# Expert 0's first part cut at 256 columns and five slices in place of 192 columns and six

## The chip, the cores and the metric

The kernel runs on one core of a Trainium2 chip. The metric is device time in microseconds (us), the median of several executions. One further execution was profiled; its trace gives a start and an end for every instruction of every engine. TensorE is PE in the rows (PEld is its weight load), VectorE is DVE, ScalarE is ACT, GpSimd is POOL, and SyncE, which issues plain DMAs, is SP.

## The reference

Three stages follow one another, on 4 batches of 768 tokens.

```python
for t in range(S):                       # gated linear attention, 8 heads of 48
    state = alpha[:, :, t, :, None] * state + einsum('bhd,bhe->bhde', k[:, :, t], v[:, :, t])
    y[:, :, t] = einsum('bhd,bhde->bhe', q[:, :, t], state)
...
expert_idx = argmax(x @ w_gate, axis=1)  # 8 experts, one per token, x is (3072, 384)
for e in range(E):
    h = maximum(x[mask] @ w1[e], 0.0)    # 384 -> 1024
    out[mask] = gate_w[mask, None] * (h @ w2[e])   # 1024 -> 384
...
h = x @ w_in                             # 384 -> 2048
g = h * (1.0 / (1.0 + exp(-h)))
return g @ w_out                         # 2048 -> 384
```

## The kernel before

**Stages.** The attention runs first, batch by batch. While the last batch is in work, the routing of the first three is known; the kernel uses that to start expert 0 early. Then come experts 0 to 7, the other seven in an order by their token counts, and then the dense layer.

**One slice of an expert.** The hidden 1024 columns are cut into 8 slices of 128 (`NF`). For a slice `t`, `F1(t, c0, c1)` makes the first products: nine matmuls (three 128-row pieces of the input, three terms each, because every operand is kept as a high part and a low part), each over the token columns `c0` to `c1`. ScalarE then writes the high part of the result, `hh` (L1276), and VectorE the low part, `hl` (L1278). `S1(t, c0, c1, between)` makes the second products: three output blocks `dc` of three matmuls. `between` holds steps that are put into PE's order behind the blocks `dc` 0, 1 and so on.

**Expert 0 in two parts.** A first part covers the first `CA` token columns, which can be gathered from the rows of the first three batches (`gather_a`, two indirect DMAs of POOL, `xg<-x_d,gidx_a`). It runs for the first `part` slices while the last batch is still being routed: its logits are turned, chosen, ranked, and turned into a list of tokens (`pt`, L884, on PE; `tab` and `gidx`, L894 and L895, on VectorE). Then the rest of expert 0's tokens is gathered (`gather(0, ...)`, `xg<-x_d,gidx`). The second part covers the columns from `CA` on for the same slices, and all columns for the slices that are left. With `part = NF - 2` and `CA = 192` that is six slices of 192 columns, the same six again on the rest, and two slices on all. The width of the rest follows the token count: `sized` branches to the smallest of the widths in `ARMS[0] = [424, 448]` that holds it.

**Tiles of tokens.** The gathered rows are turned by PE 128 at a time (`x_tile`, `x_rows`: three transposes `xt` or `both` at L373, the high part `xh` by ScalarE at L377, the low part `xl` by VectorE at L378). Tile 0 and the first 64 rows of tile 1 are turned in the last attention step; the other rows of tile 1 (its first 64 columns are skipped), tile 2 and tile 3 in the first part's last slices. VectorE also turns the counts into an order of the experts (`turns`, L902 to L919) and the lists into that order (`in_turn`, L925 to L932).

**Order.** Each engine runs its instructions in the order in which the program writes them; waits between engines are by semaphores. Before the second part, `hold()` has VectorE clear the ends of three PSUM banks (`hp`, L1263); the second part's first product writes the first of them.

Of the kernel before, what the change touches and what calls it, by code (L numbers as in the profile page):

```python
# [33 lines left out]
NF = DFF // 128  # L34
# [11 lines left out]
    [344, 356, 368, 384],  # L46
    [326, 342, 354, 370],
]
CA = 192
NTILE = NT // 128  # L50
RING = 5
TB = NTILE // B
# [187 lines left out]
def gla_moe_kernel(  # L240
# [32 lines left out]
    def bank(i, shape, name):  # L273
        if i > 1:
            return ps.tile(shape, F32, tag=f"B{i}", name=name)
        if "t" not in both:
            both["t"] = two_banks("both")
        n = 1
        for x in shape[1:]:
            n *= x  # L280
        t = both["t"][: shape[0], i, 0:n]
        return t.rearrange("p (a b) -> p a b", a=shape[1]) if len(shape) == 3 else t
# [60 lines left out]
    def w_rest(t, eng=nc.vector):  # L343
        hi, lo = wslot[slot1(t)]
        eng.tensor_tensor(lo, raw.pop(t), hi.bitcast(F32), op=ALU.subtract)  # L345

    def w_split(t, eng=nc.vector):
        w_cast(t)
        w_rest(t, eng)
# [12 lines left out]
    def gather_rows(x, src, idx, i, n):  # L362
        nc.gpsimd.indirect_dma_start(  # L363
            out=x[:n],
            out_offset=None,
            in_=src,
            in_offset=bass.IndirectOffsetOnAxis(ap=idx[:n, i : i + 1], axis=0),
        )

    def x_rows(g, xs, kt, r0, n, t):  # L370

        for kc in range(KD):
            nc.tensor.transpose(  # L373
                t[:, kc, :n].bitcast(F32R), g[:n, kc * 128 : (kc + 1) * 128].bitcast(F32R), identr[:n, :n]
            )
        xh, xl = (x[:, :, 128 * kt + r0 : 128 * kt + n] for x in xs)
        nc.scalar.copy(xh, t[:, :, r0:n])  # L377
        nc.vector.tensor_tensor(xl, t[:, :, r0:n], xh.bitcast(F32), op=ALU.subtract)  # L378
# [26 lines left out]
    with actx:  # L405
# [528 lines left out]
        def rows(b, c):  # L934
            t = bank(xbank(), [128, 4, PA], "Xt")
            for i in range(4):
                nc.tensor.transpose(t[:, i, :], xb[b][:, i, c * CH : (c + 1) * CH], ident[:PA, :PA])  # L937
            xr = xp.tile([128, 4, 2, D], F32, tag="xr", name="xr", bufs=4)
            src = bass.AP(tensor=t.tensor, offset=t.offset, ap=[t.ap[0], [PA, 4], [64, 2], [1, D]])
            nc.scalar.activation(xr, src, AF.Copy, scale=gate[b][:, c : c + 1])  # L940
            r0 = b * S + c * CH
            nc.sync.dma_start(x_d[r0 : r0 + CH, :], xr.rearrange("p i h e -> p (i h e)"))

        def gather_a():
            nc.vector.tensor_scalar(gidx_a, tab[:, 0:2], float(NT - S - 1), None, op0=ALU.min)
            nc.vector.tensor_scalar(fl[:, 3:4], carry[0:1, 0:1], float(CA), None, op0=ALU.is_lt)
            for kt in range(2):
                gather_rows(XG[kt], x_d[: NT - S], gidx_a, kt, min(128, CA - 128 * kt))

# [86 lines left out]
        for p in range(NP + 1):  # L1036
# [49 lines left out]
            if not on:  # L1086
                x_rows(XG[0], XS[0], 0, 0, 128, bank(2, [128, KD, 128], "xt"))
                x_rows(XG[1], XS[0], 1, 0, CA - 128, bank(0, [128, KD, 128], "xt"))
                w_rest(1)
# [40 lines left out]
    with mctx:  # L1130
# [5 lines left out]
        def gather(e, kts=range(4)):  # L1136
            if e < E:
                for kt in kts:
                    if 128 * kt < CAPS[e]:
                        gather_rows(XG[kt], x_d, gidx, 4 * e + kt, min(128, CAPS[e] - 128 * kt))  # L1140

        def x_tile(e, kt, r0=0, bk=7):
            if e < E and 128 * kt < CAPS[e]:
                n = min(128, CAPS[e] - 128 * kt)
                x_rows(XG[kt], XS[e % 2], kt, r0, n, bank(bk, [128, KD, 128], "xt"))
# [99 lines left out]
        def F1(t, c0, c1, mid=()):  # L1245
            F1_bank(t, c0)
            F1_products(t, c0, c1, mid)
            F1_inner(t, c0, c1)
# [8 lines left out]
        def hold():  # L1257

            HB[0] = -1
            for i in HBS:  # L1260
                held.append(bank(i, [128, CAP], "hp"))
            for t in held:
                nc.vector.memset(t[:, min(ARMS[0]) - CA :], 0.0)  # L1263

# [46 lines left out]
        def S1(t, c0, c1, between=()):  # L1311
            S1_products(t, c0, c1, S1_begin(t, c0), between)

        def S1_begin(t, c0):
            if t == 0 and c0 == 0:
                for dc in range(KD):
                    yb[dc] = bank(dc, [128, CAP], "yb")
            return hq.pop((t, c0))

        def S1_products(t, c0, c1, inner, between=()):  # L1320
            f = t % NF
            wh, wl = wslot[slot1(t)]
            hh, hl = inner
            for dc in range(KD):
                c = 384 + dc * 128
                i = 0
                for a, b_ in ((wh, hh), (wl, hh), (wh, hl)):
                    nc.tensor.matmul(  # L1328
                        yb[dc][:, c0:c1],
                        lhsT=a[:, c : c + 128],  # L1330
                        rhs=b_[:, : c1 - c0],
                        start=(f == 0 and c0 == 0 and i == 0),
                        stop=(f == NF - 1 and i == 2),
                    )
                    i += 1
                if dc < len(between):
                    between[dc]()
# [4 lines left out]
        digits, hots, invert, add = last_tb  # L1342
        row = [lambda c=c: rows(b, c) for c in range(NC)]
# [5 lines left out]

        F1(0, 0, CA, [last["l_turn"], last["l_rows"], l_max, w_diff, *last["weigh"]])  # L1350
        for step in choose:
# [4 lines left out]
            3: [last["turns"]],  # L1356
            4: [last["in_turn"]],
        }
        part = NF - 2
        seq = [(t, CA, CAPS[0]) for t in range(part)] + [(t, 0, CAPS[t // NF]) for t in range(part, E * NF)]  # L1360
        for t in range(part):
            if t == 2:
                add()
                nc.vector.tensor_copy(regs[:, 8:9], carry[:, 0:1])
                w_split(4)
                gather(0, (1, 2, 3))
            if t == 3:
                w_split(5)
            if t + 1 < part:
                F1(t + 1, 0, CA)  # L1370
            for step in beside.get(t, []):
                step()
            if t == part - 2:
                x_tile(0, 1, CA - 128)
            if t == part - 1:
                x_tile(0, 2, bk=4)
            S1(t, 0, CA, ([row[2], ranks_and, row[4]], [lambda: None, invert])[t] if t < 2 else [])
            if t == 0:
                row[5]()
                for step in placed:  # L1380
                    step()
        HBS.append(3)
        hold()
        x_tile(0, 3)
        for t in range(4, 6):
            next_load()
        soon = [6, 7]
# [329 lines left out]
```

## Time and profile before

| | |
|---|---|
| median of 3 runs | 756.24 us (756.05 to 758.76) |
| the profiled execution | 755.89 us, of which its span is 753.9 us |
| PE busy | 741.4 us, 98% of the span |
| granted TensorE clock | 0.999 of full speed over the span |
| first part of expert 0 | from about 126.8 to 146.1 us of the span |

Times in rows are counted from the start of the span. PE is busy nearly all the time, so a stretch of PE that grows or shrinks shows in the total; where PE stands idle in this part of the program, the row after the gap says in brackets how long and for whom.

### The profile page before, as it was taken

To read this page: it belongs to the slowest core of one execution; us is meant where nothing else is said; L and a number is where in the kernel's file an instruction comes from. 1 tells how busy PE (TensorE), PEld (TensorE's weight loads), DVE (VectorE), ACT (ScalarE), POOL (GpSimd) and SP (SyncE) were. 2 spreads that over 40 slices of the span, in tenths; PEclk is the share of its full clock that TensorE was granted. 3 is DMA by queue.
4 is the path that set the end of the run, shared out by engine and by line. 5 is a ranking of instruction groups with operands and counts; after the bars stand their busy time and mean duration, and the time that the engine had idled before them with its cause. 6 is when DMAs were issued, how large, how long until landed. Compare 5 with 4: busy or idle time off the path is not lost.

```text
span 753.9 us, 13462 instructions
## 1 busy us (share of the span) xinstructions
PE 741.4 (98%) x5018; PEld 681.7 (90%) x5018; DVE 464.8 (62%) x779; ACT 366.5 (49%) x685; POOL 163.9 (22%) x206
## 2 busy tenths in 40 slices
PE   8999999999999999999999999999999999999996
PEld 6888888999999999998999999999999999899996
DVE  8999986758778788988786424433342433334222
ACT  2656566445556555656444334544554545324222
POOL 6774321422224223112121200200020020002002
PEclk9999999999999999999999999999999999999999
DMA  9798994544665566563201200030030000001001
GB/s 239 196 225 220 228 275 152 168 143 154 190 198 180 178 191 209 183 188 111 83 24 38 78 19 1 33 83 19 1 110 25 20 30 13 1 1 43 1 0 47
DMA packets 41803, 81.00 MB, mean 107 GB/s; under 512 B 5696, under 2 KB 19999, under 8 KB 41704
## 3 DMA queue, kind: packets, MB, share of 16 engines
q1 hardware_dynamic: 37704, 67.60, 31.1%
q0 software_dynamic: 4000, 12.03, 5.2%
q8 instruction: 68, 1.11, 0.6%
q14 instruction: 31, 0.25, 0.1%
HBM read 68.04 MB, written 9.47 MB: 103 GB/s over the span
## 4 chain that ended last, share of the span: by engine, by line
PE 87%; issue 4%; DVE 3%; ACT 2%; DMA 2%; POOL 1%; POOLq 0%; SPq 0%; DVEq 0%; ACTq 0%
PE hp L1238 37%; PE both L1535 12%; PE ob L1535 12%; PE both L1328 9%; PE yb L1328 4%; PE Ap L607 2%; PE Yp L690 2%; PE Yp L705 2%; PE Lw L535 1%; DMA x_d<-xr 1%; PE xt L373 1%; PE Tp L595 1%; ACT Sb L679 1%; PE Xt L937 1%; PE U L643 1%
## 5 line engine op out<-in xcount | busy, mean ns | idle before, releaser
L1238 PE MATMUL hp<-xh,wh 128*128 128x512 f32 (+10 forms) x498 | 179.9, 364 | 0.4 <-ACT xh L377 0.4
L1238 PE MATMUL hp<-xh,wl 128*128 128x512 f32 (+10 forms) x498 | 179.7, 363 | 0.0
L1512 DVE TENSOR_TENSOR sg<-hp,sg 128x512 f32<-128x512 f32 (+1 forms) x97 | 66.5, 686 | 128.4 <-ACT sg L1511 127.9
L1238 PE MATMUL hp<-xl,wh 128*128 128x512 f32 (+10 forms) x498 | 127.1, 363 | 0.0
L1511 ACT ACTIVATE sg<-hp 128x512 f32<-128x512 f32 (+1 forms) x97 | 57.6, 594 | 118.3 <-PE hp L1238 113.4
L1238 PEld LDWEIGHTS hp<-xh,wh 128*128 128x128 f32 x498 | 93.6, 188 | 11.7 <-issue 0.6
L1238 PEld LDWEIGHTS hp<-xh,wl 128*128 128x128 f32 x498 | 93.7, 188 | 10.5
L1238 PEld LDWEIGHTS hp<-xl,wh 128*128 128x128 f32 x498 | 90.1, 188 | 11.8
L1557 POOL DMA_INDIRECT out_dram<-o,sidx x24 | 23.3, 972 | 275.4 <-ACT o L1555 270.9
L1165 POOL TENSOR_TENSOR wl<-dx,wh 128x384 fp32r<-128x384 f32 x32 | 39.4, 1232 | 166.4 <-ACT wh L1162 166.4
L345 DVE TENSOR_TENSOR wl<-raw,wh 128x768 fp32r<-128x768 f32 x64 | 65.1, 1019 | 8.6 <-ACT wh L341 8.2
L1276 ACT ACTIVATE hh<-hp 128x464 fp32r<-128x464 f32 (+9 forms) x70 | 34.0, 487 | 72.3 <-PE hp L1238 64.9
L341 ACT CAST wh<-raw 128x768 fp32r<-128x768 f32 x64 | 52.0, 831 | 8.6 <-DMA raw<-in_wt_dram 8.5
L1523 DVE TENSOR_TENSOR hl<-sg,hh 128x512 fp32r<-128x512 f32 x49 | 33.9, 693 | 35.6 <-ACT hh L1522 34.2
L1278 DVE SCALAR_TENSOR_TENSOR hl<-hp,hh 128x464 fp32r<-128x464 f32 (+9 forms) x70 | 38.0, 549 | 28.7 <-ACT hh L1276 28.6
L1522 ACT CAST hh<-sg 128x512 fp32r<-128x512 f32 x49 | 30.4, 621 | 49.9 <-DVE sg L1512 38.3
L1523 DVE TENSOR_TENSOR xl<-sg,xh 128x512 fp32r<-128x512 f32 (+1 forms) x48 | 32.7, 681 | 31.7 <-ACT xh L1522 23.3
L1328 PE MATMUL both<-hh,wh 128*128 128x396 f32 (+9 forms) x140 | 47.5, 339 | 0.0
L1522 ACT CAST xh<-sg 128x512 fp32r<-128x512 f32 (+1 forms) x48 | 29.3, 611 | 35.1 <-DVE sg L1512 35.1
L1328 PE MATMUL both<-hl,wh 128*128 128x396 f32 (+9 forms) x140 | 45.8, 327 | 0.5 <-DVE hl L1278 0.5
L1328 PE MATMUL both<-hh,wl 128*128 128x396 f32 (+9 forms) x140 | 45.7, 326 | 0.0
L363 POOL DMA_INDIRECT xg<-x_d,gidx x29 | 33.5, 1155 | 42.6 <-PE xt L373 18.2
(366 smaller groups left out, 1640.8 us busy)
## 6 DMA issues: line engine op xcount, KB each, us to landing
raw<-in_wt_dram SPq DMA_DIRECT2D x64, 384.0 KB, 3.8
raw<-in_w_dram SPq DMA_DIRECT2D x32, 384.0 KB, 3.8
raw<-in_alpha_dram SPq DMA_DIRECT2D x16, 336.0 KB, 3.2
x_d<-xr SPq DMA_DIRECT2D x24, 192.0 KB, 2.8
E<-in_q_dram SPq DMA_DIRECT2D x18, 144.0 KB, 5.0
E<-in_k_dram SPq DMA_DIRECT2D x18, 144.0 KB, 3.5
E<-E POOLq DMA_DIRECT2D x18, 114.0 KB, 6.4
E<-in_q_dram SPq DMA_DIRECT2D x4, 336.0 KB, 8.7
```

Source lines behind the costliest of these rows:

```text
L341: nc.scalar.copy(wslot[slot1(t)][0], raw[t])
L345: eng.tensor_tensor(lo, raw.pop(t), hi.bitcast(F32), op=ALU.subtract)
L1165: nc.gpsimd.tensor_tensor(r["lo"], r["x"], r["hi"].bitcast(F32), op=ALU.subtract)
L1238: nc.tensor.matmul(hp, lhsT=a[:, kc * 128 : (kc + 1) * 128], rhs=x[:, kc, c0:c1], start=(i == 0), stop=(i == 8))
L1276: nc.scalar.activation(hh[:, :n], hp, AF.Relu)
L1278: nc.vector.scalar_tensor_tensor(hl[:, :n], in0=hp, scalar=0.0, in1=hh[:, :n].bitcast(F32), op0=ALU.max, op1=ALU.subtract)
L1328: nc.tensor.matmul(yb[dc][:, c0:c1], lhsT=a[:, c : c + 128], rhs=b_[:, : c1 - c0], start=(f == 0 and c0 == 0 and i == 0), stop=(f == NF - ...
L1511: nc.scalar.activation(sg[:, z], hp[:, z], AF.Sigmoid)
L1512: nc.vector.tensor_tensor(sg[:, z], hp[:, z], sg[:, z], op=ALU.mult)
L1522: nc.scalar.copy(hh[:, z], sg[:, z])
L1523: nc.vector.tensor_tensor(hl[:, z], sg[:, z], hh[:, z].bitcast(F32), op=ALU.subtract)
L1535: nc.tensor.matmul(yb[tt], lhsT=a[:, tt * 128 : (tt + 1) * 128], rhs=b_[:, 384:768], start=(f == 0 and i == 0), stop=(f == NF2 - 1 and i = ...
```

## The change

`CA` goes from 192 to 256, and the first part from six slices to five (`part = NF - 3`). Tile 1 is now gathered as 128 rows by `gather_a` and turned once, in the attention's last step (`min(128, CA - 128)`, `x_rows(XG[1], ..., 0, CA - 128, ...)`, both unchanged in the text). `gather(0, ...)` fetches two tiles in place of three. Tile 3 is turned behind the first block of the last second products, and so before `hold()`. The list of pairs of slices that follows has 64 entries as before, five of them narrow in place of six.

```diff
-CA = 192
+CA = 256
...
-        part = NF - 2
+        part = NF - 3
         seq = [(t, CA, CAPS[0]) for t in range(part)] + [(t, 0, CAPS[t // NF]) for t in range(part, E * NF)]
         for t in range(part):
             if t == 2:
                 add()
                 nc.vector.tensor_copy(regs[:, 8:9], carry[:, 0:1])
                 w_split(4)
-                gather(0, (1, 2, 3))
+                gather(0, (2, 3))
...
-            if t == part - 2:
-                x_tile(0, 1, CA - 128)
+            among = [row[2], ranks_and, row[4]] if t == 0 else [lambda: None, invert] if t == 1 else []
             if t == part - 1:
                 x_tile(0, 2, bk=4)
-            S1(t, 0, CA, ([row[2], ranks_and, row[4]], [lambda: None, invert])[t] if t < 2 else [])
+                among = [lambda: x_tile(0, 3)]
+            S1(t, 0, CA, among)
             if t == 0:
                 row[5]()
                 for step in placed:
                     step()
         HBS.append(3)
         hold()
-        x_tile(0, 3)
```

VectorE, before, from the `hl` of slice 4's first products to the clearing of the banks (`xl_108` is expert 0's low part, `128x3x64` a tile of 64 rows):

```order
L1278 SCALAR_TENSOR_TENSOR hl<-hp,hh 128x192
L902 SCALAR_TENSOR_TENSOR key<-carry,keys 128x8
...
L919 CAST regs<-rk 128x8
L1278 SCALAR_TENSOR_TENSOR hl<-hp,hh 128x192
L925 TENSOR_TENSOR mt<-tab,turn 128x256
L931 TENSOR_REDUCE ttab<-mt 128x32
L932 TENSOR_SCALAR gidx<-ttab 128x28
L378 TENSOR_TENSOR xl_108<-xt,xh_107 128x3x64
L378 TENSOR_TENSOR xl_108<-xt,xh_107 128x3x128
L1263 MEMSET hp 128x232 x3
L378 TENSOR_TENSOR xl_108<-xt,xh_107 128x3x64
```

VectorE at the same place in the change:

```order
L1278 SCALAR_TENSOR_TENSOR hl<-hp,hh 128x256
L902 SCALAR_TENSOR_TENSOR key<-carry,keys 128x8
...
L919 CAST regs<-rk 128x8
L925 TENSOR_TENSOR mt<-tab,turn 128x256
L931 TENSOR_REDUCE ttab<-mt 128x32
L932 TENSOR_SCALAR gidx<-ttab 128x28
L378 TENSOR_TENSOR xl_108<-xt,xh_107 128x3x128
L378 TENSOR_TENSOR xl_108<-xt,xh_107 128x3x64
L1263 MEMSET hp 128x296 x2
```

The `hl` of slice 5 and the turn of tile 1's second half are gone; the low part of tile 3 now stands ahead of the clearing, and all of it still behind `turns` and `in_turn`.

PE, before, at the end of the first part (in brackets what an instruction waits for; `both` and `yb` are the banks of the second products):

```order
L1328 MATMUL yb<-hl,wh_2027 128x192
L373 MATMUL xt<-identr,xg_2042 128x64 [waits DMASW6_49,DVE_49]
L373 MATMUL xt<-identr,xg_2042 128x64 x2
L1289 TENSOR_LOAD regs [waits DVE_49]
L1289 ISA x2
L1295 COMPARE_AND_BRANCH
L1238 MATMUL hp<-xh_107,wh_98 128x232 [waits DVE_49,Activation_49]
...
L1238 MATMUL hp<-xl_108,wh_98 128x232 [waits DVE_49]
```

PE at the same place in the change:

```order
L373 MATMUL xt<-identr,xg_2041 128x128 [waits DMASW4_49,PE_49]
...
L373 MATMUL xt<-identr,xg_2042 128x64 [waits DMASW5_49,PE_49]
L373 MATMUL xt<-identr,xg_2042 128x64 x2
L1328 MATMUL both<-hh,wh_2025 128x256
...
L1328 MATMUL yb<-hl,wh_2025 128x256
L1289 TENSOR_LOAD regs [waits DVE_49]
L1289 ISA x2
L1295 COMPARE_AND_BRANCH
L1238 MATMUL hp<-xh_107,wh_98 128x168 [waits DVE_49,Activation_49]
```

Tile 3's transposes moved up by six matmuls; the second part's first product, 168 columns wide, has one wait for VectorE at its head, and the later wait for the low part, at the `xl` products, is gone.

## Rows read from the trace of the kernel before

**Rows 1.** The page, busy time by engine (us, share of the span, instructions)

```profile
PE 741.4 (98%) x5018; PEld 681.7 (90%) x5018; DVE 464.8 (62%) x779; ACT 366.5 (49%) x685; POOL 163.9 (22%) x206
```

**Rows 2.** Busy time in stretches of the span, granted clock as PEclk

```profile
core 0: us, PE busy (x) PEld busy (x) DVE busy (x) ACT busy (x) POOL busy (x), PEclk, DMA share, GB/s
126.80:146.10 19.30, 18.70 (x170) 16.91 (x169) 13.84 (x49) 9.13 (x21) 4.55 (x5) 1.00 0.44 143
146.10:165.00 18.90, 18.88 (x151) 18.78 (x152) 10.93 (x29) 8.70 (x17) 7.85 (x8) 1.00 0.52 164
165.00:333.00 168.00, 168.00 (x982) 165.46 (x981) 137.00 (x233) 95.51 (x179) 45.39 (x38) 1.00 0.59 185
```

**Rows 3.** The chain in order of time: start, length, what

```profile
125.00 0.35 PE both L373 x3
...
136.55 0.60 PE pt L884 x6
...
137.55 1.00 PE hp L1238 x9
...
145.75 0.33 ACT xh L377
...
146.12 3.28 PE hp L1238 x27
...
151.69 2.01 PE hp L1238 x18
...
156.25 2.72 PE hp L1238 x18
...
360.58 4.12 PE hp L1238 x18
```

**Rows 4.** POOL's timeline, the gathers (start, length)

```profile
122.14 0.94 POOL L363 DMA_INDIRECT xg<-x_d,gidx_a  x1 [0.30 <-issue]
138.51 0.96 POOL L363 DMA_INDIRECT xg<-x_d,gidx  x1 [15.44 <-DVE wl L345]
139.78 1.68 POOL L363 DMA_INDIRECT xg<-x_d,gidx  x1 [0.30 <-issue]
```

**Rows 5.** DMA issues, windows at 122, at 138.5 and at 142 us

```profile
xg<-x_d,gidx_a POOLq DMA_INDIRECT x1, 2.7
...
xg<-x_d,gidx POOLq DMA_INDIRECT x1, 4.0
...
xg<-x_d,gidx POOLq DMA_INDIRECT x1, 2.7
```

**Rows 6.** Busy tenths of the DMA engines, 122 to 126 us, 0.1 us each

```profile
DMA  0000099952395210046844100000003399679799
```

**Rows 7.** VectorE's timeline, 137 to 147 us

```profile
137.41 0.17 DVE L895 TENSOR_SCALAR gidx<-tab 128x4 uint32<-128x4 f32 x1
...
140.97 0.36 DVE L1278 SCALAR_TENSOR_TENSOR hl<-hp,hh 128x192 fp32r<-128x192 f32 x1 [0.33 <-ACT hh L1276]
141.25 0.16 DVE L902 SCALAR_TENSOR_TENSOR key<-carry,keys 128x8 f32<-128x8 f32 x1
...
142.72 0.17 DVE L919 CAST regs<-rk 128x8 int32<-128x8 f32 x1
142.98 0.36 DVE L1278 SCALAR_TENSOR_TENSOR hl<-hp,hh 128x192 fp32r<-128x192 f32 x1
...
144.35 0.18 DVE L932 TENSOR_SCALAR gidx<-ttab 128x28 uint32<-128x28 f32 x1
144.44 0.99 DVE L378 TENSOR_TENSOR xl<-xt,xh 128x192 fp32r<-128x192 f32 x2
145.47 0.75 DVE L1263 MEMSET hp<- 128x232 f32 x3
```

**Rows 8.** ScalarE's timeline, 142 to 147 us

```profile
143.08 0.32 ACT L377 CAST xh<-xt 128x192 fp32r<-128x192 f32 x1
```

**Rows 9.** PEld's loads of the first products, one line, 127 to 146 us (ns min/median/max)

```profile
L1238 PEld LDWEIGHTS hp<-xh,wh x18: 186/192/192, 128.2 to 141.8; 128*128 128x128 f32 x18
```

## The prediction

> **What bounds the kernel now.** I read the page first, then the stretches of the span, then the chain in order of time around expert 0's first part, and last the timelines of the engines that PE waits for there. The page says PE: it is busy 98% of the span [rows 1]. The stretches say where it isn't. From 165 us on, and already from 146.1 to 165, PE is busy in all but 0.02 us of its time; in the first part of expert 0, from 126.8 to 146.1, it lacks 0.6 us of 19.3 [rows 2]. So this is a kernel in which a microsecond more of PE work behind 146 us shows as a microsecond of time, and in which the first part can be shortened only as far as PE isn't made to wait there for somebody else. The clock is granted in full in all these stretches (1.00, the 2.4 GHz level) and plays no part.
>
> The chain shows what PE's time is made of. Nine first products of 192 columns take 1.00 us, 111 ns each; eighteen of 232 columns take 2.01 us, 112 ns each [rows 3]. Forty columns more cost nothing: both widths stand on a floor. The eighteen at 156.25 are nine of 232 and nine of 424 columns and take 2.72 us, so a 424-wide one is (2.72 - 9 x 0.112) / 9 = 0.190 us; one of 512 columns is 4.12 / 18 = 0.229 us [rows 3]. Above the floor a column costs (229 - 190) / 88 = 0.44 ns.
>
> At the end of the first part PE waits until 146.12: the chain goes through ScalarE's `xh` of tile 3 at 145.75 [rows 3]. VectorE is hardly less late there. ScalarE has the high part of tile 1 ready at 143.08 + 0.32 = 143.40 [rows 8], but VectorE comes to its low part only at 144.44, because `turns` (141.25 to 142.89) and the steps of `in_turn` (up to 144.53) stand ahead of it in its order; the clearing of the banks then runs from 145.47 [rows 7].
>
> **The change, part by part.** The sum goes along the time at which the second part's first product can start: 146.12 before [rows 3]. All of PE's work behind it is then compared.
>
> *Tile 1 gathered whole.* The second gather of `gather_a` starts at 122.14 and lands 2.7 us later, at 124.84 [rows 4, 5]; PE's transposes of it are in the chain at 125.00 [rows 3], so there is next to no slack. It now moves 128 rows. POOL's own time is the same (0.94 us for 64 rows, 0.96 for 128 [rows 4]). Bounds for the landing: nothing, and the 4.0 us that the 128-row gather at 138.51 took, that is +1.3 us [rows 4, 5]. In between, the busy tenths show the first gather's 128 rows as a burst of ten slices and the second's 64 rows as one of six, of 0.1 us each [rows 6], so 64 rows more are 0.4 us. I take **+0.4 us**, being the row of this very place. All of the last attention step, the logits and the routing stand behind it.
> By the Trainium skill ("DMA: Bandwidth & Descriptors", section on the anatomy of one SWDGE DMA) a DMA takes about 2.0 us plus its bytes over 436 GB/s; by an estimate from that page 98 KB more cost 0.23 us, and the total would be 0.2 us lower. Its 2.2 us for 64 rows is under the 2.7 us measured here, so the trace decides.
>
> *256 columns in place of 192.* No row has this width. Bounds: the floor of 112 ns, and the 190 ns of 424 columns. The line through 424 and 512 gives 190 - 168 x 0.44 = 116 ns, which I take: **+4 ns** a matmul. Ahead of the list of tokens (`pt`), 27 are on the path (six ahead of the turned logits, 21 between the routing's last transposes and `pt`; while the routing runs on VectorE and ScalarE the others only fill PE): +0.11 us. Behind `pt` come 30 up to the end of slice 4's first products: +0.12 us.
> The Trainium skill ("TensorE: Matmul & The Clock Gate", section on the back-to-back issue gap) gives an isolated matmul N/2.4 + 2.5 ns; by an estimate from that page 256 columns are 109 ns, under this trace's floor, and the total would be 0.2 us lower. For 512 columns it gives 216 ns where the row has 229, so I stay with the line.
>
> *VectorE's queue at the end of the first part.* This is where the gain should come, and where I think it goes. Before, `hl` of slice 4 ends at 140.97 + 0.36 = 141.33 [rows 7]. Now it ends later by 0.4 + 0.11 + 0.12, and by about 0.06 each for `hh` and `hl` that are a third wider (an estimate from the 0.36 us of this `hl`): 142.08. Behind it, in VectorE's order: `turns`, 1.56 us (141.33 to 142.89); `in_turn`, 1.19 us (from 143.34, the end of slice 5's `hl`, which is now gone, to 144.53); the low parts of tiles 2 and 3, a pair of the same sizes as the pair at 144.44, 0.90 us (144.53 to 145.43); the first clearing, 0.04 + 0.25 us, with 296 columns for 232 some 0.07 more [rows 7]. That makes 142.08 + 1.56 + 1.19 + 0.90 + 0.36 = 146.09, and with 0.04 us to start, **146.13**. The second part's first product waits for the clearing at its head. So the start stays where it was.
>
> *What PE does meanwhile.* It loses a slice: 18 matmuls of 111 ns, 2.0 us, and one turn of a half tile. `pt` ends at 137.15 + 0.51 = 137.66 [rows 3]. With 39 matmuls of 116 ns it is at tile 2's transposes at 142.2. Tile 2's gather starts 0.93 us behind `gidx` as before (137.58 to 138.51), at 139.02, and lands 2.7 to 4.0 us later, 141.7 to 143.0; tile 3's starts 1.27 us behind it and lands from 143.0 on [rows 4, 5, 7]. PE is through by about 144.6 and then stands for 1.5 us, where it stood for 0.4 before. Any wait for tiles 2 and 3 up to that size is hidden under VectorE's queue.
>
> *Slice 5 goes whole to the second part.* Its 18 matmuls there have 424 columns in place of 232: 18 x (190 - 112) = **+1.40 us**. The other five narrow slices have 168 columns for 232, both on the floor (192 and 232 are [rows 3]): nothing. PE is full there [rows 2], so all of this shows.
>
> *Steps at nothing.* The 128-row transposes, `xh` and `xl` of tile 1 in the attention's last step lengthen ScalarE and VectorE by 0.1 to 0.2 us where both wait for PE; one gather less on POOL brings tiles 2 and 3 up to 1.27 us sooner, which counts for nothing as long as VectorE's queue is the later one.
>
> Sum: 755.89 (the profiled execution) + 0.01 + 1.40 = 757.3. The median of the runs is 0.35 above the profiled one, so **757.5 us**, 0.2% up. What a measurement of this kernel can tell from no change is about 0.5%, 3.8 us: no change.
>
> **The rivals.** *Early start.* The clearing doesn't hold the product's head (it writes columns from 168 on, the product those below): then only the seventh matmul waits, for the low part at 145.73, the first six take 0.67 us, and the start comes at 145.1: 1.0 us less, 756.5. For it: the columns don't overlap in the narrower arm. Against it: in the order of the change the one wait for VectorE stands at the head. With a gather that lands no later it would be 756.1.
>
> *Late gather.* The whole tile 1 lands 1.0 to 1.3 us later rather than 0.4, as the 4.0 us row has it [rows 5]; this moves everything: 0.6 to 0.9 more, 758.3. For it: two of the three landings shown are 2.7 and both are of 64 rows. Against: the burst in [rows 6].
>
> *Wide matmul off the floor*, the slower side. A load of weights takes 192 ns [rows 9] and is hidden only because the next one begins under the matmul. If 256 columns broke this overlap, a narrow matmul would cost the 190 ns of the nearest row. Ahead of slice 4's `hl` stand 45 first and 27 second products, 72 x 74 ns = 5.3 us: about 762.8, 0.9% slower. It decides from (3.8 - 1.3) / 72 = 35 ns on, a pace of about 150 ns. Against it: 192 and 232 columns share one pace under the same loads, and 424 lies on a line with 512.
>
> *The change doesn't do what it says*, in that the shorter first part starts nothing earlier, is my forecast itself.
>
> **How the numbers follow.** Forecast 0.62 (757.0 to 758.0); early start 0.18; late gather 0.14; wide matmul 0.04; 0.02 for what I don't see. The range that leaves out no more than 2 in 10 goes from the early start with its lower bound to the late gather with a run's spread: 755.6 to 759.2. Faster by over 0.5% would need 752.4, where none of these ends: 0.01. Slower by over 0.5% is the wide matmul and a part of the unseen: 0.05. Same: 0.94.
>
> **What would show it.** Right: VectorE without a gap from slice 4's `hl` to the first clearing, the second part's first product within 0.3 us behind that clearing, near 146.1, and PE idle for 1 to 2 us ahead of it; 256-wide nines of about 1.04 us; tile 1's transposes about 0.4 us later; one more nine of 424 columns. Wrong: a first product that starts ahead of the clearing (early start); nines of 1.3 us or more (wide matmul); a gap of PE ahead of tile 1's transposes of a microsecond (late gather); or PE waiting for tiles 2 and 3 beyond VectorE's queue.

## The result, and the profile after

| | before | changed |
|---|---|---|
| median | 757.26 us (22 runs, 755.0 to 761.4) | 766.71 us (22 runs, 757.1 to 771.4) |
| ratio | | 1.0089, 95% interval 1.007 to 1.0108 |
| granted TensorE clock, mean over a run | 0.997 to 1.0 (its runs beside the experiments) | 0.999 to 1.0 in 4 runs, 0.984 to 0.988 in 18 |
| the profiled execution | 755.89 us | 768.97 us, span 767.3 us, clock 0.986 |

The change makes the kernel 0.9% slower (9.4 us by the medians), where no change was forecast. The 22 runs fall in two groups with nothing between: four at 757.1, 757.8, 758.7 and 759.3 us, near the forecast of 757.5, and eighteen from 763.5 us on, with a median of 767.2. The mean clock parts them without exception. (Four of the eighteen, from 769.0 us on, are left out of the ratio as disturbed; their clock is that of the other fourteen.)

First the page of the changed kernel: PE's busy time as in [rows 1], and the granted clock in 40 slices of the span, 19 us each.

```profile
PE 749.3 (98%) x4997; PEld 690.1 (90%) x4997; DVE 464.5 (61%) x777; ACT 366.3 (48%) x683; POOL 160.4 (21%) x205
...
PEclk9999999869999999999999999999999999999999
```

PE is busy 7.9 us longer with 21 instructions fewer. The clock line says where to look: one slice of 8 and one of 6, between 134 and 173 us, and nothing else. The stretches of that place, as in [rows 2]:

```profile
core 0: us, PE busy (x) PEld busy (x) DVE busy (x) ACT busy (x) POOL busy (x), PEclk, DMA share, GB/s
126.80:144.00 17.20, 17.13 (x165) 15.46 (x164) 12.02 (x37) 10.18 (x22) 1.91 (x2) 1.00 0.48 152
144.00:148.20 4.20, 2.67 (x20) 2.11 (x19) 3.87 (x14) 0.80 (x2) 0.81 (x1) 1.00 0.12 28
148.30:168.70 20.40, 20.34 (x95) 20.28 (x96) 7.05 (x22) 4.43 (x10) 5.93 (x8) 0.50 0.43 140
168.80:200.00 31.20, 31.20 (x175) 29.97 (x174) 20.43 (x35) 15.84 (x29) 4.82 (x5) 1.00 0.42 131
```

In the 4.2 us at the end of the first part PE works 2.67 us. Then the granted clock is 0.50, the lower of the two levels (1.2 GHz), for 20.4 us, although PE is busy in 20.34 of them. PE's timeline at both ends of this stretch (start, length, line, shape, and in brackets the idle time ahead of a row and who ended it):

```profile
130.61 0.38 PE L1238 MATMUL hp<-xh,wh 128*128 128x256 f32 x1
...
145.55 0.42 PE L373 MATMUL xt<-identr,xg 128*128 128x128 f32 x3 [0.98 <-DMA xg<-x_d,gidx]
...
147.37 0.28 PE L1328 MATMUL yb<-hl,wh 128*128 128x256 f32 x1
148.36 0.48 PE L1238 MATMUL hp<-xh,wh 128*128 128x168 f32 x1 [0.71 <-DVE hp L1263]
148.64 0.41 PE L1238 MATMUL hp<-xh,wl 128*128 128x168 f32 x1
148.85 0.41 PE L1238 MATMUL hp<-xh,wh 128*128 128x168 f32 x1
...
166.88 0.63 PE L1238 MATMUL hp<-xh,wh 128*128 128x424 f32 x1
...
168.37 0.53 PE L1238 MATMUL hp<-xh,wh 128*128 128x424 f32 x1
168.72 0.37 PE L1238 MATMUL hp<-xh,wl 128*128 128x424 f32 x1
...
175.96 0.35 PE L1238 MATMUL hp<-xh,wh 128*128 128x420 f32 x1
```

PE stands 0.98 us for the gathered rows of tile 2, works 2.1 us, stands 0.71 us for VectorE's clearing, and its next product already runs at the lower level. From there a product of 168 columns starts every 0.21 us (148.64 to 148.85), nearly twice the 111 ns of [rows 3]. This goes on through all the narrow slices. Only with the first products of 424 columns, from 166.88 on, does the clock come back, at 168.7.

What it costs is read between two points that both kernels have: the second part's first product and the first product of the next expert, 420 columns wide. In the changed kernel that is 175.96 - 148.36 = 27.60 us. The timeline of before has

```profile
128.16 0.36 PE L1238 MATMUL hp<-xh,wh 128*128 128x192 f32 x1
...
162.83 0.35 PE L1238 MATMUL hp<-xh,wh 128*128 128x420 f32 x1
```

and so 162.83 - 146.12 = 16.71 us [rows 3]. Of the 10.9 us more, 1.4 were forecast for slice 5; some 9.4 are the clock. The two groups of runs differ by nearly as much: their medians, 758.3 and 767.2 us, are 9 us apart.

VectorE's timeline of the changed kernel at the same place, as in [rows 7]:

```profile
143.95 0.42 DVE L1278 SCALAR_TENSOR_TENSOR hl<-hp,hh 128x256 fp32r<-128x256 f32 x1 [0.48 <-ACT hh L1276]
144.29 0.16 DVE L902 SCALAR_TENSOR_TENSOR key<-carry,keys 128x8 f32<-128x8 f32 x1
...
147.03 0.81 DVE L378 TENSOR_TENSOR xl<-xt,xh 128x384 fp32r<-128x384 f32 x2
147.91 0.94 DVE L1263 MEMSET hp<- 128x296 f32 x3
```

No row after the first has a wait: the queue runs through from slice 4's `hl` to the clearing, as the prediction described it. From the first product of expert 0 to the second part's first product the changed kernel takes 148.36 - 130.61 = 17.75 us, the kernel before 146.12 - 128.16 = 17.96 us.

### The profile page after: what moved, and what is told of

Its sections match the earlier page's. It is cut to its first block, busy times and chain, and to the rows that moved or that the text cites. A ratio compares the mean times of both kernels' runs of the same rounds, so it can differ in the third digit from the quotient of the medians.

```text
span 767.3 us, 13412 instructions
## 1 busy us (share of the span) xinstructions
PE 749.3 (98%) x4997; PEld 690.1 (90%) x4997; DVE 464.5 (61%) x777; ACT 366.3 (48%) x683; POOL 160.4 (21%) x205
## 4 chain that ended last, share of the span: by engine, by line
PE 81%; DMA 6%; DVE 5%; issue 4%; ACT 2%; SPq 1%; POOL 1%; POOLq 0%; DVEq 0%; ACTq 0%
PE hp L1238 37%; PE both L1534 12%; PE ob L1534 12%; PE both L1328 9%; PE yb L1328 4%; DMA E<-E 2%; PE Ap L607 1%; DVE Pf L562 1%; DMA E<-in_q_dram 1%; PE Yp L690 1%; DMA a__148<-in_alpha_dram 1%; PE xt L373 1%; PE Yp L705 1%; DMA x_d<-xr 1%; DVE Rv L580 1%
## 5 line engine op out<-in xcount | busy, mean ns | idle before, releaser
L1238 PE MATMUL hp<-xh,wh 128*128 128x512 f32 (+10 forms) x495 | 183.0, 371 | 0.7 <-DVE hp L1263 0.7
L1238 PE MATMUL hp<-xh,wl 128*128 128x512 f32 (+10 forms) x495 | 182.6, 370 | 0.0
L1238 PE MATMUL hp<-xl,wh 128*128 128x512 f32 (+10 forms) x495 | 128.7, 369 | 0.0
L1238 PEld LDWEIGHTS hp<-xh,wh 128*128 128x128 f32 x495 | 95.5, 193 | 12.2 <-issue 1.5
L1238 PEld LDWEIGHTS hp<-xh,wl 128*128 128x128 f32 x495 | 95.6, 193 | 10.6
L1238 PEld LDWEIGHTS hp<-xl,wh 128*128 128x128 f32 x495 | 91.7, 192 | 11.9
L1328 PE MATMUL both<-hh,wh 128*128 128x404 f32 (+9 forms) x138 | 48.4, 351 | 0.0
L1328 PE MATMUL both<-hl,wh 128*128 128x404 f32 (+9 forms) x138 | 46.6, 338 | 0.4 <-DVE hl L1278 0.4
L1328 PE MATMUL both<-hh,wl 128*128 128x404 f32 (+9 forms) x138 | 46.5, 337 | 0.0
L363 POOL DMA_INDIRECT xg<-x_d,gidx x28 | 30.8, 1098 | 55.9 <-PE xt L373 25.2
```

Source lines behind the costliest of these rows:

```text
L1238: nc.tensor.matmul(hp, lhsT=a[:, kc * 128 : (kc + 1) * 128], rhs=x[:, kc, c0:c1], start=(i == 0), stop=(i == 8))
L1328: nc.tensor.matmul(yb[dc][:, c0:c1], lhsT=a[:, c : c + 128], rhs=b_[:, : c1 - c0], start=(f == 0 and c0 == 0 and i == 0), stop=(f == NF - ...
```

## The experiments

Two things meet at the place where the clock falls: PE has stood longer than before, and what follows is 168 columns wide where it was 232. The first theory was the first alone: the stands let the clock fall. The rivals were the narrow products alone, and the five slices with their tight gathers. Times in the text are medians; "before" is the kernel before in runs beside them on the same chip.

**Both stands filled** (`filled`). The changed kernel with matmuls of ones that nothing reads, on 128 columns, put into the two stands.

```diff
+        def fill(n):
+            t = bank(3, [128, 128], "fill")
+            for _ in range(n):
+                nc.tensor.matmul(t, lhsT=ones, rhs=ones, start=True, stop=True)
...
+                fill(20)
                 x_tile(0, 2, bk=4)
...
+        fill(18)
         HBS.append(3)
         hold()
```

> The change, with 20 and 18 matmuls of ones by ones (128 columns, result unused) put into PE's order where it waits at the end of the first part: ahead of tile 2's transposes, and behind the last second products. Theory (PE's standing at the end of the first part is what brings TensorE's clock down to its lower level for 20 us): PE has work there, the granted clock stays at full speed, and the time is that of the sum in the prediction, 757 to 758.5 us. Rival (the clock falls because the second part's products have only 168 columns, so the array has less to do between loads of weights): those products are the same here, the clock falls as in the change, about 766 us.

766.68 us (9 runs, before 757.27; ratio 1.0095, 1.0058 to 1.0131): four runs of 759.7 to 761.4 us at a clock of 0.996 to 1.0, five of 766.7 to 768.6 us at 0.988 to 0.991. Five of nine against eighteen of 22 doesn't show that the filling made the fall rarer. What the fallen runs say of the stands can be read only from a profile of one of them (below).

**256 columns, but six slices** (`six256`). All of the change except the number of slices; its second part is 168 columns wide six times.

```diff
-        part = NF - 3
+        part = NF - 2
```

> The change with six slices in the first part in place of five, all else as in the change: 18 matmuls of 256 columns more (2.1 us) ahead of the tiles of the last batch. Theory (standing): the gathers and VectorE are done when PE comes, PE stands for less than 0.5 us, the clock stays at full speed, 756 to 758 us. Rival (168 columns): six narrow slices of 168 columns in the second part, more than in the change; the clock falls, 766 us or more.

757.22 us (10 runs, before 757.27; ratio 0.9994, 0.9974 to 1.0013), clock 0.996 to 1.0 in all of them. The stretch of the second part in its profile:

```profile
145.20:164.00 18.80, 18.64 (x149) 18.49 (x150) 10.64 (x30) 8.02 (x17) 7.38 (x9) 1.00 0.53 170
```

PE stood only once, 0.34 us, ahead of that stretch. Narrow products alone don't bring the clock down here. The wider columns, tile 1 gathered whole and tile 3 turned early together cost nothing that shows.

**192 columns, but five slices** (`five192`). The kernel before with `part = NF - 3`, and nothing else of the change.

> The kernel before with five slices in the first part in place of six, 192 columns kept. Theory (standing): PE comes 2 us earlier to tile 1's transposes, whose gather lands at 142.5 us, and stands some 1.9 us there and some 0.8 us ahead of the second part; the clock falls for about 20 us and the time is 766 to 769 us. Rival (168 columns): the second part has 232 columns as before, the clock stays, about 757.5 us.

760.19 us (10 runs, before 757.27; ratio 1.0031, 1.0012 to 1.0049), clock 0.993 to 1.0. The stretches of its profile:

```profile
142.00:149.00 7.00, 4.42 (x37) 3.88 (x36) 5.69 (x18) 1.45 (x4) 4.37 (x4) 1.00 0.50 146
149.00:165.00 16.00, 16.00 (x128) 15.66 (x128) 9.36 (x25) 6.68 (x14) 6.50 (x8) 1.00 0.52 160
```

PE stood for 2.6 of the 7.0 us at the end of the first part, more than in the changed kernel (1.12, 0.45, 0.21 and 0.81 us), and the clock stayed at 1.00. The time expected of the stands (766 to 769 us) did not come: stands alone don't cost 9 us here, and neither do five slices. Shorter falls are likely in other runs of it, since in six of the ten the mean clock was 0.993 to 0.995. Its second part is 232 columns wide.

**A longer stand in the kernel before** (`idle4`). Four clearings of a 128x512 tile by VectorE ahead of the clearing of the banks.

```diff
+        late_clear = mp.tile([128, TM], F32, tag="sg", name="late_clear", bufs=2)
+        for _ in range(4):
+            nc.vector.memset(late_clear, 0.0)
         HBS.append(3)
         hold()
```

> The kernel before with four clearings of an unused tile of 512 columns on VectorE ahead of the clearing of the PSUM banks; PE's own work is unchanged. VectorE is 1.2 to 2.1 us later there and PE stands for 1.3 to 2.2 us in place of 0.4. Theory (standing): the clock falls, 765 to 769 us, some 10 us more than the 0.9 to 1.8 us that the delay itself costs. Rival (168 columns): only the delay, 757 to 758 us.

761.78 us (10 runs, before 757.27; ratio 1.0047, 1.0025 to 1.0068), clock 0.993 to 0.999. PE's timeline in its profile:

```profile
150.27 0.34 PE L1238 MATMUL hp<-xh,wh 128*128 128x232 f32 x1 [2.67 <-DVE hp L1263]
...
151.00 0.42 PE L1238 MATMUL hp<-xh,wh 128*128 128x232 f32 x1
151.21 0.41 PE L1238 MATMUL hp<-xh,wl 128*128 128x232 f32 x1
```

The stretches from there on:

```profile
150.60:153.90 3.30, 3.30 (x18) 3.30 (x17) 0.93 (x6) 0.38 (x1) 0.65 (x1) 0.50 0.35 103
154.10:170.00 15.90, 15.90 (x130) 15.80 (x129) 9.23 (x22) 7.56 (x16) 5.09 (x5) 1.00 0.38 120
```

The stand, 2.67 us, does bring the clock down. But it is back after some 3.4 us, within products of 232 columns, where the changed kernel's 168 columns left it low for 20.4. The 765 to 769 us expected of the stand alone did not come. So the theory was changed: **a stand lets the clock fall, and it then stays low through a second part of 168 columns, but not through one of 232.** The next four runs were made for that.

**The same stand, ahead of 168 columns** (`six256_idle4`). The insertion of `idle4` in `six256`.

> Six slices on 256 columns (755 to 761 us, clock full in all its runs) with four clearings of a 128x512 tile by VectorE put ahead of the clearing of the banks, so that TensorE stands some 2.5 us there, as it did in the kernel before with the same insertion (761.8 us, clock at its lower level for 3.4 us). Theory A (a stand of TensorE at the end of the first part lets the clock fall, and products over 168 columns at the lower level don't bring it back, while products over 232 columns do): the clock stays at half through all the 168-wide products of the second part, some 15 to 20 us, and the time is 766 to 770 us. Theory B (only the standing counts, whatever the width behind it): half clock for 3.4 us as with 232 columns, 761 to 763 us. Theory C (it takes five slices, since there the stretch of narrow products is longer or the gathers later): no long fall, below 762 us.

769.46 us (4 runs, 768.3 to 772.7, before 756.84; ratio 1.0162, 1.0121 to 1.0203), clock 0.979 to 0.985 in every run. The stretches of its profile:

```profile
147.30:149.30 2.00, 0.00 (x0) 0.00 (x0) 1.48 (x4) 0.00 (x0) 1.39 (x3) 1.00 1.01 382
149.50:173.20 23.70, 23.04 (x107) 22.91 (x108) 8.90 (x26) 5.48 (x12) 4.61 (x6) 0.50 0.26 83
```

By its timeline PE stood 2.86 us here, 2.67 in `idle4`, for the same clearing. The clock was low for over 23 us against 3.4. With six slices and no wait for a gather, this is the changed kernel's fall made by hand. `idle4` differs from it in the width of the second part, and also in the rest that comes with `CA` (256 columns in the first part, tile 1 gathered whole, tile 3 turned early); the next run keeps these and changes the width.

**The changed kernel, 232 columns in the second part** (`wide232`). The second products of the first part leave out their last 64 columns, and the second part takes them; the first products of the first part keep all 256.

```diff
-                nc.vector.memset(t[:, min(ARMS[0]) - CA :], 0.0)
+                nc.vector.memset(t[:, min(ARMS[0]) - CA + 64 :], 0.0)
...
-        seq = [(t, CA, CAPS[0]) for t in range(part)] + ...
+        seq = [(t, CA - 64, CAPS[0]) for t in range(part)] + ...
...
-            S1(t, 0, CA, among)
+            S1(t, 0, CA - 64, among)
```

> The changed kernel, but with the second products of expert 0's first part over columns 0 to 191 only and its second part over columns 192 to 424 in both products: 232 columns instead of 168, at the same pace when the clock is full (111 to 112 ns each). The first products of the first part still run over 256 columns, so the output is the reference's, and the standing of TensorE before the second part is that of the changed kernel (about 0.98 and 0.7 us). Theory A (the clock falls by the standing, and stays low because 168 columns don't raise it): it falls at most for a few us, 757 to 761 us, most runs at a clock above 0.993. Theory B (the standing alone makes the fall of 20 us): as the changed kernel, 766 to 767 us, clock 0.984 to 0.988 in most runs. Theory C (the 256-wide first products of the first part bring the clock down): also 766 to 767 us.

760.21 us (10 runs, 756.9 to 763.4, before 756.84; ratio 1.004, 1.0018 to 1.0063), clock 0.994 to 1.0 in all runs. By PE's timeline in its profile the second stand was longer than both of the changed kernel together:

```profile
148.90 0.34 PE L1238 MATMUL hp<-xh,wh 128*128 128x232 f32 x1 [1.83 <-DVE hp L1263]
```

and the stretches behind it are

```profile
149.80:153.00 3.20, 3.20 (x18) 3.20 (x17) 0.86 (x5) 1.00 (x3) 2.27 (x3) 0.50 0.88 314
153.20:170.00 16.80, 16.62 (x122) 16.20 (x122) 8.62 (x22) 6.36 (x14) 4.51 (x5) 1.00 0.38 122
```

More columns in the second part, and some 6 us less time than the changed kernel (3.4 us over before in place of 9.4): the fall is there and short. So 256 columns in the first part's first products don't keep the clock low. (The first part's second products are 192 columns wide here, the one other difference.)

One run of a version is profiled, and only there can the length of a fall be read. For the others there is an estimate from the mean clock: in the changed kernel 0.986 over 767 us lacks 10.7 us of full clock, or 21 us at half of it, near the 20.4 us read. The lowest mean of `idle4`, `five192` and `wide232`, 0.993 over 760 us, lacks 5.3 us, or some 11 us at half. So some of these runs were probably low for longer than 3.4 us, and none for as long as the changed kernel.

**The changed kernel, VectorE's queue cut** (`early_turns`). `turns` and `in_turn` one slice earlier, slice 5's weights split in the second part.

```diff
-            if t == 3:
-                w_split(5)
...
-            3: [last["turns"]],
-            4: [last["in_turn"]],
+            2: [last["turns"]],
+            3: [last["in_turn"]],
...
-        for t in range(4, 6):
-            next_load()
-        soon = [6, 7]
+        next_load()
+        soon = [5, 6, 7]
```

> The changed kernel with VectorE's queue ahead of the second part cut: the turns and their sums one slice earlier, and slice 5's weights split in the second part instead of ahead of its slice 3. TensorE then stands only for the gathered rows (about 1 us), and the second stand of 0.7 us ahead of the second part's first product is gone or under 0.3 us. Theory A with the stands summed up: the falls become rarer or stop, below 762 us in most runs. Theory that one stand of 1 us or the narrow products behind it are enough: 764 to 768 us in most runs, as the changed kernel.

758.14 us (10 runs, 756.3 to 759.4, before 756.84; ratio 1.0011, 0.9993 to 1.0029), clock 0.996 to 1.0 in all runs. The waits of PE from 126 to 149 us in the changed kernel (in all, times, longest):

```profile
PE xt L373 <- DMA xg<-x_d,gidx: 1.0, 1, 1.0
PE Yp L690 <- ACT xb L719: 0.9, 1, 0.9
PE hp L1238 <- DVE hp L1263: 0.7, 1, 0.7
```

and in this one:

```profile
PE xt L373 <- DMA xg<-x_d,gidx: 1.0, 1, 1.0
PE hp L1238 <- DVE hp L1263: 0.4, 1, 0.4
```

The stretch of its second part:

```profile
147.00:165.00 18.00, 18.00 (x139) 17.80 (x139) 10.00 (x27) 7.24 (x15) 6.70 (x7) 1.00 0.49 156
```

And three rows of PE's timeline, the first one expert 0's first product:

```profile
129.21 0.39 PE L1238 MATMUL hp<-xh,wh 128*128 128x256 f32 x1
...
146.66 0.32 PE L1238 MATMUL hp<-xh,wh 128*128 128x168 f32 x1 [0.35 <-DVE hp L1263]
...
164.82 0.35 PE L1238 MATMUL hp<-xh,wh 128*128 128x420 f32 x1
```

The wait for the gathered rows is the same 1.0 us, the narrow products are the same, and half of the second stand is gone: the clock holds in ten of ten runs, where it fell in 18 of 22. (The wait for `xb` in the first list ends at 125.97 us, in the attention's last step; the clock was at 1.00 in the 17 us from 126.8 us on.) That the shorter stand does it, and nothing else that moved with VectorE's steps, is the likely reading and not shown by itself. From the second part's start to the next expert it takes 164.82 - 146.66 = 18.16 us. Against the 16.71 us of before, slice 5 whole costs 1.45 us; against the 27.60 us of the changed kernel, the low clock cost 9.44 us.

**Filling and 232 columns together** (`filled_wide`).

> The last kernel but one of the narrow widths changed (second part over 232 columns) together with the earlier filling of both stands by 38 products of ones that nothing reads. With the filling alone the second part over 168 columns still had the low clock in five of nine runs. Theory A (the 168 columns keep the clock at its lower level, whatever brings it down): no run below a clock of 0.993, 757 to 760 us. Theory B (something else in the changed kernel than standing or width, the filling itself for one): five of nine runs again near 767 us.

759.37 us (10 runs, 756.8 to 760.8, before 756.84; ratio 1.0026, 1.0009 to 1.0043), clock 0.996 to 1.0. With the wider products no run of the filled kernel falls for long; with 168 columns five of nine did. So the filling itself isn't the cause of those five.

**A fallen run of `filled`, profiled** (`filled_b`, `filled_c`: the kernel of `filled`, one run each).

> The kernel with both stands filled again, for a profile of one of its runs near 767 us (five of nine had such times, at a clock of 0.988 to 0.991). Theory A (with 168 columns in the second part any stand near it lets the clock fall, and the columns keep it low): the low stretch begins in the second part, behind a stand that the filling doesn't cover, lasts until the 424-wide products, some 15 to 20 us, and its 168-wide products take about 213 ns. Theory B (the filling itself brings the clock down): it falls while the products of ones run or within the first 256-wide slices, before the second part. A run near 760 us tells nothing of it.

> The same once more, for the same profile; the expectation is that of the run ahead of it.

769.49 and 768.73 us (before 758.38), clock 0.990 and 0.988: both fell. From the first one's timeline of PE:

```profile
154.14 0.32 PE L1328 MATMUL both<-hh,wh 128*128 128x168 f32 x1 [2.23 <-DVE yb L1398]
```

Its stretches:

```profile
144.00:151.50 7.50, 7.46 (x83) 7.05 (x83) 4.26 (x16) 0.80 (x2) 3.42 (x4) 1.00 0.49 167
151.50:155.10 3.60, 1.37 (x14) 1.26 (x13) 1.63 (x6) 1.65 (x4) 1.52 (x3) 1.00 0.25 80
155.20:168.70 13.50, 13.50 (x62) 13.31 (x62) 4.50 (x15) 2.58 (x6) 1.91 (x2) 0.50 0.34 103
```

Both stands are filled (7.46 us busy of 7.50), and the clock holds through them and through the first 168-wide products. Then PE stands 2.23 us in the second part, the clock falls behind that, and stays low up to the 424-wide products. The filled kernel had got a new stand further on. The second profile has the same order with stands of 0.59 and 0.72 us (and one of 0.48 us still at tile 2's rows), and a clock of 0.50 from 151.9 to 169.0 us. What makes the new stand is ScalarE: in the first profile its `hh` of the second part's first slice starts at 153.00, when the nine products that it reads are through by 149.7. Why it is late there isn't shown.

**Only the second stand filled** (`fill_second`). The changed kernel with `fill(18)` alone.

> The changed kernel with only the second stand filled, by 18 products of ones behind the last second products of the first part; the wait of about 1 us for the gathered rows stays. With the second stand taken away by an earlier start of VectorE's queue instead, the clock held in all ten runs (758.1 us). Theory A (the second stand decides): 757 to 760 us, clock above 0.995 in nearly all runs. Rival (products of ones on 128 columns don't count as the stand's end, as in the run with both filled): 764 to 768 us in half of the runs or more.

758.32 us (10 runs, 756.1 to 762.5, before 758.38 in 13 runs; ratio 0.9997, 0.997 to 1.0024), clock 0.998 to 1.0 in all runs. The fall is gone here too. In its profile PE waited 0.88 us for the clearing behind the filling, and no wait for tile 2's rows was there; so the one stand left was about half of the two of the changed kernel. It is the second stand, which the filling was to take away; the run therefore doesn't show which of the two counts.

All of it in one table (difference of the medians from before, clock over the runs). The columns go by the stands in the profiles, added up from the end of the first part into the second, one profile of each version and for `filled` the two fallen ones:

| | PE stands 0.3 to 1.4 us | PE stands 1.7 to 2.9 us |
|---|---|---|
| second part 232 wide | before: 0.997 to 1.0; `filled_wide` +2.5, 0.996 to 1.0 | `idle4` +4.5, `five192` +2.9, `wide232` +3.4: 0.993 to 1.0 |
| second part 168 wide | `six256` 0.0, `early_turns` +1.3, `fill_second` -0.1: 0.996 to 1.0 | changed kernel +9.5, `six256_idle4` +12.6, `filled` +9.4: 0.979 to 0.991 in their fallen runs |

No version beats the kernel before: where the clock holds in `early_turns`, five slices pay 1.45 us in the second part and win about half a microsecond (129.21 to 146.66, that is 17.45 us, from the first product to the second part in `early_turns`; 17.96 before).

## Why the prediction was wrong

**The step that failed** is the sentence "The clock is granted in full in all these stretches (1.00, the 2.4 GHz level) and plays no part", together with "Any wait for tiles 2 and 3 up to that size is hidden under VectorE's queue". The first is a reading of the kernel before, carried over to a kernel in which the same text has PE stand for 1.5 us. In VectorE's queue that stand is indeed hidden, and the second part did not start later. But it isn't free: with 168 columns behind it, the clock fell to 0.50 for 20.4 us, which cost 9.4 us in the profiled run, and the clock was low in 18 of 22 runs. A stand of PE has two prices, its length and what the clock does afterwards, and the prediction counted the first. No rival had the clock either; it went into the 0.02 for what was not seen.

**What held.** *VectorE's queue sets the start*: no gap from `hl` to the clearing, PE's first product 0.45 us behind the clearing's start, 3.99 us from the end of slice 4's `hl` (143.95 + 0.42 = 144.37) to that product (148.36), where the sum has 146.13 - 142.08 = 4.05. *PE stands for 1.5 us*: 0.98 + 0.71 = 1.69, in two pieces, since tile 2's rows came 4.5 us behind the start of their gather and not 2.7 to 4.0. *Slice 5 whole, +1.40*: 1.45, measured where the clock holds. *Narrow slices at 168 columns, nothing*: right at the full clock (`six256`), and wrong at the lower level, as above. Where the clock held, the time was close to the forecast: 757.1 to 759.3 us in four runs of the changed kernel, 758.1 and 758.3 with shorter stands. The sum started low: its 756.24 for before came from three runs, where 22 give 757.26, and 757.3 and 0.35 make 757.65, not 757.5. On 757.26 its 1.41 us more would have been 758.7; the median of the four is 758.3.

**Sizes.** *256 columns*: the chain has for one nine of the first part

```profile
142.42 1.09 PE hp L1238 x9
```

121 ns each, where 116 were forecast from the line through 424 and 512 columns; 0.3 us over 57 of them. The Trainium skill ("TensorE: Matmul & The Clock Gate", section on the back-to-back issue gap) has an isolated matmul at N/2.4 + 2.5 ns, by an estimate from it 109 ns for this width; the row disagrees, and by more than the line does. *Tile 1 gathered whole, +0.4*: can't be read in the profiled run, because the attention ahead of it ended later, its transposes start 2.4 us later than in [rows 3], and PE waits there for ScalarE and not for the gather. `wide232` has the same gather, and PE waits for it there:

```profile
128.20 0.42 PE L373 MATMUL both<-identr,xg 128*128 128x128 f32 x3 [0.41 <-DMA xg<-x_d,gidx_a]
xg<-x_d,gidx_a POOLq DMA_INDIRECT x1, 3.0
```

The 128 rows landed 3.0 us after their issue, 0.3 more than the 2.7 of [rows 5]; the forecast had 0.4. `six256`, which has the gather too, is level with before.

**The rivals.** The early start didn't come: the first product waits for the clearing in the changed kernel. The late gather, which needed 1.0 to 1.3 us more for tile 1, didn't come in `wide232` (0.3). The wide matmul stays on its line (121 ns, far from the 150 from which it would decide).

**What stays open.** The runs show which stands and which width go with a long fall in this part of the kernel, not why. The width by itself is no rule: in `filled` the clock came back under narrower products of the attention (last section). Why the clock stayed in four of the changed kernel's 22 runs isn't shown, and neither is a stand length from which it falls: 1.12, 0.45, 0.21 and 0.81 us in one execution (`five192`) left it alone, 0.98 and 0.71 us in another did not.

## What to carry to other kernels

A granted clock of 1.00 in the profile of a tuned kernel is a result of how PE is kept busy, and a change that makes PE stand has to be priced twice: the stand, and the work behind it at half speed until the clock comes back. Ask what follows the stand: in expert 0's second part, products of 232 columns had the clock back in some 3.4 us in two profiles, and products of 168, at which PE was busy nearly without a gap, did not have it back in 13 to 23 us in four. The cure was off PE: moving VectorE's steps out of one queue shortened one wait from 0.71 to 0.35 us, and the median fell by some 8 us.

## What the runs showed of the hardware

- The lower clock level outlasted 20.34 us of PE work in a stretch of 20.40 us (changed kernel) and 23.04 of 23.70 (`six256_idle4`), nearly all of it on 168 columns, and ended within 3 us of the first products of 424 columns. Under products of 232 columns it ended after some 3.4 us, twice. The Trainium skill ("TensorE: Matmul & The Clock Gate", Part 1) says that the low level is the default and that activity releases it. The 232-column rows agree; in the 168-column rows PE worked almost without a gap and the clock stayed at 0.50, and there the measurement decides.
- At the lower level 168 and 232 columns cost the same, 0.21 us a product (148.64 to 148.85 in the changed kernel, 151.00 to 151.21 in `idle4`), as at the full clock they share 111 to 112 ns. So the products under which the clock came back cost no more apiece.
- The profiled execution of `filled` lost the clock much earlier, behind stands of 0.25 and 0.85 us in the attention's last step, for some 3.3 us, and had it back before expert 0's second part. PE's timeline and the stretches:

```profile
123.86 0.91 PE L690 MATMUL Yp<-E,Sb 112*112 112x128 f32 x6 [0.85 <-ACT xb L719]
...
127.53 0.42 PE L705 MATMUL Yp<-Am,v__1735 128*48 128x128 f32 x1
127.55 0.42 PE L702 MATMUL Yp<-Am,v__1735 128*48 128x128 f32 x1
127.74 0.42 PE L705 MATMUL Yp<-Am,v__1735 128*48 128x128 f32 x1
...
128.11 1.79 PE L736 MATMUL Lp<-xb,wgs 112*32 112x384 f32 x16
125.40:128.70 3.30, 3.30 (x29) 2.55 (x32) 2.02 (x4) 1.58 (x4) 0.00 (x0) 0.50 0.44 128
146.60:165.00 18.40, 17.82 (x150) 17.18 (x149) 10.44 (x30) 6.42 (x14) 8.20 (x9) 1.00 0.54 175
```

What ran while the clock was low there were products of 128 columns, two of them every 0.21 us (127.53 to 127.74), and at the end the first `Lp` products; the clock was back at about 128.7 us. So the clock also came back under products narrower than the 168 columns that left it low elsewhere: these are smaller products at a faster pace, and which difference counts isn't shown.
